# Linear attention and two feed-forwards: halves by batch, y written to the input tile by 32-column matmuls

## The chip, the cores and the metric

One core of a Trainium2 chip. The metric is the device time of one launch in microseconds (us), as the median of several runs; below one per cent, two such medians of this kernel can hardly be told apart.

## The reference, cut to what matters

```python
for t in range(S):                                   # S = 768, 4 batches, 8 heads, 48 channels
    state = alpha[:, :, t, :, None] * state + np.einsum('bhd,bhe->bhde', k[:, :, t], v[:, :, t])
    y[:, :, t] = np.einsum('bhd,bhde->bhe', q[:, :, t], state)
...
h = x @ w_in                                         # x: y as 3072 tokens x 384; w_in 384 x 2048, float64
g = (a[0] + a[1]*h + a[2]*h*h + a[3]*h**3) / (1.0 + np.abs(b[0])*np.abs(h) + np.abs(b[1])*h*h + 1e-6)
x = g @ w_out                                        # 2048 x 384
...
h = x @ w_in2                                        # 384 x 1024, then softmax times h, a norm, and @ w_out2
```

## The kernel before, in words

The sequence is cut into 6 chunks of 128 steps. Attention works on a chunk in two halves, `i = 2c + g`: in half `g` stand four of the eight heads, of all four batches. For a half, `a_dve` (halves 2 to 11; `a_turn` for halves 0 and 1) makes q and k scaled by the running product of alpha, on VectorE (DVE), and sends them through DRAM (`qk_d`, `kb_d`) to `qks` and `kns`. Then `a_pe` runs on TensorE (PE), head pair by head pair (`p` = 0, 1): scores `sc` (L396), copied and masked to `A` (L403, L404); y from the state matrix `Sbd` (L413, from chunk 1 on) and from `A` and v (L421, heads at output columns 0 and 64); at the end of the half the state update `u` (L446). A matmul of float32 is two instructions in the trace, so 4 matmuls of L413 are 8 there.

y lies head by head in PSUM, with 48 rows of every 64 in use. The feed-forward wants the 384 features in order on partitions, as three tiles `xt` of 128. So L427 and L428 copy y to `xp` as a high and a low part, and DMAs put its rows where they belong: in chunk 0 directly into `xt` (`x_put`, L533), later into a DRAM array `y_d` (L434), from which `x_load` (L540) fills `xt` when the chunk's feed-forward begins. `xt` has one buffer.

The first feed-forward runs in steps `u`, 16 a chunk, 96 in all: `m_up` does 9 matmuls of 512 columns (L555) to `hp`, then a rational function on ACT, DVE and POOL, and `m_down` 9 matmuls (L601) four steps later. Its weights come as float64 and are converted on DVE, three instructions a tile (L491, L494, L495), for the first 16 steps; the tiles `st` and `lent` hold what is loaded. The second feed-forward (L677, L741) begins in the last chunk.

Half `i` = 2c+2 and 2c+3 of attention runs between the steps of chunk c, so halves 4 to 11 run in chunks 1 to 4. The order of instructions on each engine is fixed when the program is built, by a scheduler that simulates it; each engine then works through its list in order. All DMAs are issued by one queue, SP's, in order too: one that waits holds up those behind it.

Of the kernel before, what the change touches and what calls it, by code (L numbers as in the profile page):

```python
# [30 lines left out]
def kernel(  # L31
# [41 lines left out]
    GQ = 0  # L73
# [34 lines left out]
    def consts():  # L108
        """|b1| h^2 + |b0| |h| + QC and |a3| h^2 + s a2 h + s a1 (s the sign of a3) as (root x + beta)^2 + rest."""
# [29 lines left out]
    def network(fast):  # L139
        # ------------------------------------------------------------ attention  # L140
# [6 lines left out]
        if fast:  # L147
# [19 lines left out]
            S_c = ap_.tile([128, 2, B * 2, D], F32, name="S_c")  # L167
            Sbd = ap_.tile([128, 2, B * 2, 128], F32, name="Sbd")

        def clear():  # L170
            nc.gpsimd.memset(d1, 0.0)
            nc.gpsimd.memset(_view(d1[:], 0, [[PER, NB6 + 1]]), 1.0)
            nc.gpsimd.memset(d2, 0.0)
            nc.vector.memset(alT[:, NB6 * PER:], 0.0)
            nc.vector.memset(_view(alT[:], 0, [[PER, NB6 + 1]]), 0.0)
# [45 lines left out]
        def watch(i, ra):  # L221
            jk = ap_.tile([128, 16 * D], BF16, name="jk", tag="R")
# [11 lines left out]
        def a_load(i):  # L234
            c, g = divmod(i, 2)
            if i == 1:
                own = {
                    n: borrow(3, 2048 + 1024 * x, [16 * D + 16]) for x, n in enumerate(("ra", "rk", "rq"))
                }
            for src, nm in ((alpha, "ra"), (k, "rk"), (q, "rq")):  # L240
                t = own[nm] if i == 1 else ap_.tile([128, 16 * D + 16], F32, name=nm, tag=nm)
                if i < NPE:
                    nc.gpsimd.memset(t[:, 16 * D:], 1.0)
                for b in range(B):
                    nc.sync.dma_start(  # L245
                        out=t[32 * b:32 * b + 32, :16 * D].rearrange("p (h x) -> p h x", h=4),
                        in_=src[b, 4 * g:4 * g + 4, CH * c:CH * c + CH, :].rearrange("h (j r) d -> j h (r d)", r=4),
                    )
                raws[i, nm] = t
                yield  # L250

        def a_move(i):
            c, g = divmod(i, 2)
# [22 lines left out]
        def a_dve(i):  # L276
            ra = raws.pop((i, "ra"))
            watch(i, ra)
            transpose_in(ra, alT[:], 1, 3 * PER, PER)
            yield  # L280
# [13 lines left out]
            nc.vector.tensor_tensor(qv[1], qv[1], _view(R[:], 0, [[3 * PER, 2], [PER, 3], [1, CH]]), ALU.mult)  # L294
            yield
            kb = ap_.tile([128, 4, 192], F32, name="kb", tag="R")
            for p in range(2):
                nc.vector.transpose(
                    out=_view(kb[:], 96 * p, [[32, 3], [192, 4], [1, 32]]),
# [4 lines left out]
                out=kb_d[:].rearrange("b (j r) x -> (b j) (r x)", r=4), in_=kb[:].rearrange("p r x -> p (r x)")  # L304
# [9 lines left out]
        vns = {}  # L314

        def v_load(i):
            c, g = divmod(i, 2)
            vn = vns[i] = (
                borrow(2, 1024, [B * 192 + 16]) if i == 1
                else ap_.tile([128, B * 192 + 16], F32, name="vn", tag="vn", bufs=1)  # L320
            )
            nc.gpsimd.memset(vn[:, B * 192:], 0.0)
            for b in range(B):
                nc.sync.dma_start(
                    out=vn[:, 192 * b:192 * b + 192].rearrange("p (h d) -> p h d", h=4),
                    in_=v[b, 4 * g:4 * g + 4, CH * c:CH * c + CH, :].rearrange("h t d -> t h d"),
                )

        def a_turn(i):
# [15 lines left out]
            for p in range(2):  # L345
                al = turn(ra, p)
                P = ap_.tile([128, B, CH], F32, name="Pp", tag="P")
                R = ap_.tile([128, B, CH], F32, name="Rp", tag="R")
# [38 lines left out]
        def a_pe(i):  # L387
            c, g = divmod(i, 2)
            vt = vns.pop(i)
            hf = half(i)  # L390
            for p in range(2):
                at = []
                sc = [ps_ap.tile([128, B, CH], F32, name="sc", tag="at") for j in range(2)]
                for b in range(B):
                    for j in range(2):
                        nc.tensor.matmul(  # L396
                            sc[j][:, b, :],
                            lhsT=hf.k[p][64 * j:64 * j + D, b, :], rhs=hf.q[p][64 * j:64 * j + D, b, :],
                            start=True, stop=True,
                        )  # L400
                for j in range(2):
                    t = ap_.tile([128, B, CH], F32, name="A", tag=f"A{j}")
# [5 lines left out]
                    at.append(t)  # L408
                yield
                y = ps_ap.tile([128, B, CH], F32, name="y", tag="at")  # L410
                if c:
                    for b in range(B):
                        nc.tensor.matmul(  # L413
                            y[:, b, :], lhsT=Sbd[:, g, 2 * b + p, :], rhs=hf.q[p][:, b, :],
                            start=(b == 0), stop=False, skip_group_check=True,
                        )
                M = D if c else 64
                for b in range(B):
                    for j in range(2):
                        o = 192 * b + 96 * p + 48 * j  # L420
                        nc.tensor.matmul(  # L421
                            y[64 * j:64 * j + M, b, :], lhsT=vt[:, o:o + M], rhs=at[j][:, b, :],
                            start=(c == 0 and b == 0), stop=(b == B - 1), skip_group_check=True,
                        )
                xp = ap_.tile([128, 2, NTOK], F32R, name="xp", tag="xp")
                yf = y[:].rearrange("p b t -> p (b t)")
                nc.scalar.activation(xp[:, 0, :], yf, AF.Copy)  # L427
                marks[i, p] = nc.vector.tensor_tensor(xp[:, 1, :], yf, xp[:, 0, :].bitcast(F32), ALU.subtract)  # L428
                for j in range(2):
                    r0 = 192 * g + 96 * p + 48 * j  # L430
                    if c == 0:
                        x_put(xp, j, r0)
                        continue
                    nc.sync.dma_start(  # L434
                        out=y_d[c][r0:r0 + D, :],
                        in_=xp[64 * j:64 * j + D].rearrange("p a t -> p (a t)").bitcast(F32),
                    )
                yield
# [3 lines left out]
            for b in range(B):  # L442
                for p in range(2):
                    for j in range(2):
                        o = 192 * b + 96 * p + 48 * j
                        nc.tensor.matmul(  # L446
                            u[64 * j:64 * j + 64, 2 * b + p, :], lhsT=hf.kn[:, o:o + 64], rhs=vt[:, o:o + D],
                            start=True, stop=True, skip_group_check=True,
                        )
            if c < NCH - 1:  # L450
                Ab = hf.ends
                Sg = S_c[:, g].rearrange("p (b w) e -> p b w e", b=B)
                if c:
                    nc.vector.tensor_tensor(S_c[:, g], S_c[:, g], u, ALU.add)
                    nc.gpsimd.tensor_tensor(Sg, Sg, Ab, ALU.mult)
                else:
# [567 lines left out]
```

## Time and profile before

| what | value |
|---|---|
| runs shown | 832.57, 827.46, 832.26 us; median 832.26 |
| profiled execution, first to last instruction | 830.2 us |
| PE busy | 775.5 us (93%) |
| DVE, ACT, POOL busy | 77%, 68%, 43% |
| DMA | 118.95 MB, 52% of 16 engines' span |
| mean granted PE clock | 0.952 |

The profiled execution is 2.1 us shorter than the median of the runs. Busy time of PE is a modelled figure: matmuls overlap, and the start of the next one tells more than the length of one.

### The profile page before, as it was taken

How to read it: one execution, taken by the hardware profiler on the slowest of the kernel's cores; microseconds unless marked ns; L12 is line 12 of the kernel's file. 1: busy time of each engine (PE TensorE's matmuls, PEld its weight loads, DVE VectorE, ACT ScalarE, POOL GpSimd, SP SyncE). 2: the span in 40 equal slices, each digit the busy share in tenths (PEclk: the TensorE clock that was granted, in tenths of full speed). 3: DMA queues.
4: the chain of work that ended last, by engine and by line, in shares of the span. 5: the costliest groups of instructions: out<-in, count | busy, mean ns of one | idle time of the engine just before them, and what ended most of it. 6: DMA issues, size and time to landing. Idle time of an engine off the chain costs nothing.

```text
span 830.2 us, 12585 instructions
## 1 busy us (share of the span) xinstructions
PE 775.5 (93%) x4274; PEld 640.3 (77%) x4274; DVE 635.5 (77%) x1088; ACT 564.4 (68%) x1005; POOL 357.6 (43%) x298
## 2 busy tenths in 40 slices
PE   5884989799999999989999999999999999999986
PEld 4763867577777777777777878888888989999986
DVE  6897989989597978868797966466886799776730
ACT  2334767578778787859869787798886555455541
POOL 3245767766554354433444433242224515343331
PEclk9876879899999999989999999999999999999998
DMA  7889573573848494655648160650012643632552
GB/s 170 222 202 231 169 193 103 162 212 101 223 155 202 159 246 129 201 142 175 173 119 257 54 158 20 250 210 16 1 39 78 150 98 89 151 88 70 129 123 61
DMA packets 92201, 118.95 MB, mean 143 GB/s; under 512 B 34400, under 2 KB 63072, under 8 KB 92128
## 3 DMA queue, kind: packets, MB, share of 16 engines
q1 hardware_dynamic: 92128, 118.07, 51.9%
q8 instruction: 35, 0.57, 0.3%
q14 instruction: 38, 0.31, 0.1%
HBM read 68.46 MB, written 35.42 MB: 125 GB/s over the span
## 4 chain that ended last, share of the span: by engine, by line
PE 57%; DVE 16%; DMA 12%; SPq 6%; issue 4%; ACT 3%; POOL 2%; ACTq 0%; DVEq 0%; POOLq 0%
PE x2p L601 16%; PE hp L555 16%; PE h L677 8%; PE op L741 7%; DMA qks<-qk_d 4%; PE sc L396 4%; PE y L421 2%; DMA xt<-xp 2%; SPq L245 1%; PE y L413 1%; SPq L727 1%; DVE ft L494 1%; DMA st<-in_moe_w_out_dram 1%; DVE room L717 1%; ACT jk L702 1%
## 5 line engine op out<-in xcount | busy, mean ns | idle before, releaser
L555 PE MATMUL hp<-xt,g 128*128 128x512 f32 x720 | 194.3, 416 | 17.8 <-DMA xt<-xp 12.8
L589 POOL TENSOR_TENSOR gl<-p,gh 128x512 fp32r<-128x512 f32 x96 | 131.3, 1369 | 182.0 <-ACT gh L588 121.5
L601 PE MATMUL x2p<-gh,g 128*128 128x512 f32 x576 | 198.1, 403 | 0.0
L555 PEld LDWEIGHTS hp<-xt,g 128*128 128x128 f32 x720 | 141.2, 200 | 52.9 <-issue 9.2
L601 PEld LDWEIGHTS x2p<-gh,g 128*128 128x128 f32 x576 | 108.1, 190 | 26.7 <-issue 2.5
L601 PE MATMUL x2p<-gl,g 128*128 128x512 f32 x288 | 114.7, 398 | 0.0
L741 PE MATMUL op<-w2oh,room 128*128 128x384 f32 x384 | 102.9, 342 | 2.9 <-ACT room L732 2.2
L733 POOL TENSOR_TENSOR room<-room,room 128x1024 fp32r<-128x1024 f32 x22 | 53.7, 2441 | 102.2 <-ACT room L732 98.7
L584 DVE SCALAR_TENSOR_TENSOR w<-w,co,hp 128x512 f32<-128x512 f32 x84 | 61.9, 738 | 46.6 <-ACT hp L583 46.6
L677 PE MATMUL h<-w2ih,x 128*128 128x512 f32 x288 | 90.2, 392 | 0.0
L560 ACT ACTIVATE ah<-hp 128x512 f32<-128x512 f32 x96 | 56.9, 593 | 46.7 <-PE hp L555 45.5
L563 ACT ACTIVATE w<-ah,co 128x512 f32<-128x512 f32 x96 | 78.1, 813 | 4.4 <-DVE p L579 2.6
L581 DVE SCALAR_TENSOR_TENSOR p<-p,co,hp 128x512 f32<-128x512 f32 x84 | 61.7, 735 | 24.1 <-ACT p L562 23.9
L562 ACT ACTIVATE p<-hp,co 128x512 f32<-128x512 f32 x96 | 74.3, 774 | 1.3 <-POOL gl L589 1.3
L741 PEld LDWEIGHTS op<-w2oh,room 128*128 128x128 f32 x384 | 71.1, 191 | 4.4 <-ACT room L732 2.6
L588 ACT ACTIVATE gh<-p 128x512 fp32r<-128x512 f32 x96 | 60.1, 627 | 13.3 <-PE x2p L601 8.8
L396 PEld LDWEIGHTS sc<-qks 48*128 48x128 f32 x352 | 45.3, 205 | 30.7 <-issue 22.4
L396 PE MATMUL sc<-qks 48*128 48x128 f32 x352 | 56.1, 309 | 12.1 <-DMA qks<-qk_d 11.9
L741 PE MATMUL op<-w2ol,room 128*128 128x384 f32 x192 | 65.6, 341 | 0.0
L601 PEld LDWEIGHTS x2p<-gl,g 128*128 128x128 f32 x288 | 54.5, 189 | 12.5 <-issue 1.1
L586 DVE SCALAR_TENSOR_TENSOR p<-p,co,hp 128x512 f32<-128x512 f32 x84 | 62.0, 738 | 1.3
L677 PEld LDWEIGHTS h<-w2ih,x 128*128 128x128 f32 x288 | 53.9, 188 | 10.7
(173 smaller groups left out, 1423.6 us busy)
## 6 DMA issues: line engine op xcount, KB each, us to landing
room<-room SPq DMA_DIRECT2D x96, 128.0 KB
qk_d<-qk SPq DMA_DIRECT2D x10, 771.0 KB
st<-in_moe_w_in_dram SPq DMA_DIRECT2D x15, 512.0 KB
st<-in_moe_w_out_dram SPq DMA_DIRECT2D x20, 384.0 KB
y_d<-xp SPq DMA_DIRECT2D x40, 192.0 KB
xt<-y_d SPq DMA_DIRECT2D x12, 512.0 KB
qks<-qk_d SPq DMA_DIRECT2D x20, 257.0 KB
x_d<-x2e SPq DMA_DIRECT2D x18, 256.0 KB
```

The lines of the kernel that those rows point to most:

```text
L396: nc.tensor.matmul(sc[j][:, b, :], lhsT=hf.k[p][64 * j:64 * j + D, b, :], rhs=hf.q[p][64 * j:64 * j + D, b, :], start=True, stop=True,)
L555: nc.tensor.matmul(hp, lhsT=w[:, kt, 128 * o:128 * o + 128], rhs=xts[c, kt][:, xx, :], start=(kt == 0 and w is hi and xx == 0), stop=(kt = ...
L562: nc.scalar.activation(p, hp, AF.Square, bias=co[:, 7:8], scale=co[:, 5:6])
L563: nc.scalar.activation(w, ah, AF.Square, bias=co[:, 6:7], scale=co[:, 4:5])
L581: nc.vector.scalar_tensor_tensor(p, p, a1, hp, ALU.add, ALU.mult)
L584: nc.vector.scalar_tensor_tensor(w, w, rest, hp, ALU.add, ALU.mult)
L586: fin[u] = nc.vector.scalar_tensor_tensor(p, p, a0, hp, ALU.add, ALU.mult)
L588: nc.scalar.activation(gh, p, AF.Copy)
L589: nc.gpsimd.tensor_tensor(gl, p, gh[:].bitcast(F32), ALU.subtract)
L601: nc.tensor.matmul(x2ps[c][d], lhsT=w[:, o, 128 * d:128 * d + 128], rhs=gg, start=(f == 0 and w is hi and gg is gh), stop=(f == NF1 - 1 an ...
L677: nc.tensor.matmul(hp[:, 512 * n:512 * n + 512], lhsT=x2s[c][kt][:, x, CH * b:CH * b + CH], rhs=w2[w][:, kt, 512 * n:512 * n + 512], start ...
L741: nc.tensor.matmul(op, lhsT=x[:, 128 * f:128 * f + 128], rhs=w2[w][:, f, :], start=(f == 0 and x is hi and w == "oh"), stop=(f == NF2 - 1 ...
```

## The change

Halves are now two batches with all eight heads (`slot`), so a half yields all 384 features of 256 tokens. Scores of both head pairs come first, into four tiles `A`; then all y matmuls of the half in one block. They use 32 output columns each: a pair of heads is 96 features, three pieces of 32, and output piece `m` goes to partitions `32 (m mod 4)` of tile `m // 4`. Successive matmuls thus go to the four column groups in turn. y is then in feature order, and the copies write `xt` directly, which holds all three tiles and has two buffers. `xp`, `x_put`, `y_d` in the fast path and `x_load` go. v gets 64 columns a head with zeros behind the 48. The state lives in the diagonal blocks of `Sbd` (`S_c` goes, and the two ACT copies of L459), so the DVE and POOL updates are done in two pieces of 48 partitions. To make room, `R` and `kb` lie in `alT`, `rq` shares a tile with `ra` and is loaded after `ra` was transposed, and `jk` shares the tile of `qk`.

```diff
+        def slot(i, x):
+            c, bp = divmod(i, 2)
+            return c, 2 * bp + x // 2, 4 * (x % 2)
...
         def a_dve(i):
             ra = raws.pop((i, "ra"))
+            nc.vector.memset(_view(alT[:], PER, [[PER, NB6], [1, 2]]), 0.0)
             watch(i, ra)
             transpose_in(ra, alT[:], 1, 3 * PER, PER)
+            _run(a_load(i, ("rq",)))
...
-            R = ap_.tile([128, NB6 * PER], F32, name="R", tag="R")
-            nc.vector.tensor_tensor_scan(R[:, ::-1], alT[:, 2:][:, ::-1], d2[:, ::-1], 0.0, ALU.mult, ALU.add)
+            R = alT[:, 2:]
+            nc.vector.tensor_tensor_scan(R[:, ::-1], R[:, ::-1], d2[:, ::-1], 0.0, ALU.mult, ALU.add)
...
+            y2 = [ps_ap.tile([128, n, 2 * CH], F32, name="y", tag="at") for n in (2, 1)]
+            begun = set()
+            def put(m, x, w, r, last):
+                kt, quad = divmod(m, 4)
+                first = (kt // 2, quad) not in begun
+                begun.add((kt // 2, quad))
+                nc.tensor.matmul(
+                    y2[kt // 2][32 * quad:32 * quad + 32, kt % 2, CH * x:CH * x + CH], lhsT=w, rhs=r,
+                    start=first, stop=last, skip_group_check=True,
+                )
+            pairs = range(H // 2)
+            for x in range(2):
                 if c:
+                    for hp in pairs:
+                        g, p = divmod(hp, 2)
+                        for z in range(3):
+                            put(
+                                3 * hp + z, x, Sbd[:, bp, 2 * (2 * x + g) + p, 32 * z:32 * z + 32],
+                                hf.q[p][:, 2 * x + g, :], False,
+                            )
+                for part in ((0, 1, 3), (2,)):
+                    for hp in pairs:
+                        g, p = divmod(hp, 2)
+                        for z in part:
+                            o = 512 * x + 128 * hp + (0, 32, 48, 80)[z]
+                            put(
+                                3 * hp + (0, 1, 1, 2)[z], x, vt[:, o:o + 32], A[p, z // 2][:, 2 * x + g, :], z != 1
+                            )
+            xt = x_tile(c)
+            for z, n in enumerate((2, 1)):
+                hi, lo = (xt[:, 2 * z:2 * z + n, w, 256 * bp:256 * bp + 256] for w in range(2))
+                nc.scalar.activation(hi, y2[z], AF.Copy)
+                marks[i, z] = nc.vector.tensor_tensor(lo, y2[z], hi.bitcast(F32), ALU.subtract)
...
+                xts[c] = moe_pool.tile([128, KT, 2, NTOK], F32R, name="xt", tag="xt", bufs=2)
...
-                if f == 0 and c:
+                if f == 0 and c and not fast:
                     x_load(c)
```

The order on PE, at the end of half 3's y in chunk 0. Before: y of the second head pair, cut in two, and the state update `u` around its second part.

```order
L555 MATMUL hp<-xt,g_738 128x512 x9
L413 MATMUL y<-qks,Sbd 128x128 x4
L421 MATMUL y<-A,vn 48x128
L601 MATMUL x2p_1083<-gl,g_612 128x512
L601 MATMUL x2p_1083<-gh,g_612 128x512
L601 MATMUL x2p_1081<-gh,g_738 128x512
L601 MATMUL x2p_1081<-gl,g_738 128x512
L446 MATMUL u<-vn,kns 64x48 x11
L421 MATMUL y<-A,vn 48x128 x7
L446 MATMUL u<-vn,kns 64x48 x5
L601 MATMUL x2p_1081<-gh,g_738 128x512
```

The same half's y now:

```order
L604 MATMUL x2p_1113<-gh,g_619 128x512
L422 MATMUL y<-qks,Sbd 32x128 x12
L422 MATMUL y<-A,vns 32x128 x16
L422 MATMUL y<-qks,Sbd 32x128 x12
L422 MATMUL y<-A,vns 32x128 x16
L558 MATMUL hp<-xt,g_735 128x512 x9
```

All 56 y matmuls of the half stand together, where before each head pair had its own stretch, cut once or twice. Over halves 4 to 11 the attention matmuls stood in 75 separate blocks between feed-forward matmuls, and now in 57.

The order on SP's queue during chunk 0, while half 1 is finished and half 2 made. Before (`lent` and `st` are the landing tiles of the float64 weights):

```order
L488 DMA st<-in_moe_w_out_dram 128x384
L533 DMA xt<-xp 48x1024
L533 DMA xt<-xp 16x1024
L533 DMA xt<-xp 32x1024
L303 DMA kb_d<-kb 128x768
L245 DMA rq<-in_q_dram 32x4x192 x2
L258 DMA kns<-kb_d 128x4x192
L245 DMA rq<-in_q_dram 32x4x192
L488 DMA lent_176<-in_moe_w_in_dram 128x512
L311 DMA qk_d<-qk 128x3x514
L488 DMA st<-in_moe_w_out_dram 128x384
L533 DMA xt<-xp 48x1024 x2
```

And now:

```order
L501 DMA st<-in_moe_w_out_dram 128x384
L251 DMA rk<-in_k_dram 32x4x192
L310 DMA kb_d<-alT 128x768
L501 DMA lent_173<-in_moe_w_in_dram 128x512
L251 DMA ra<-in_alpha_dram 32x4x192
L263 DMA kns<-kb_d 128x4x192
L501 DMA st<-in_moe_w_out_dram 128x384
L251 DMA ra<-in_alpha_dram 32x4x192 x3
L318 DMA qk_d<-qk 128x3x514
L501 DMA lent_173<-in_moe_w_out_dram 128x384
L501 DMA st<-in_moe_w_in_dram 128x512
```

The `xt<-xp` rows, and what they waited for, are gone; the weight loads stand in their place.

And on DVE, between half 2 and half 3 of the new order (`alT` is now also `kb`, the source of the DMA `kb_d<-alT`):

```order
L305 STREAM_TRANSPOSE alT<-qk 128x3x4x32 x2
L276 STREAM_TRANSPOSE qk<-rq 128x4x32 x2
L508 SCALAR_TENSOR_TENSOR ft<-lent_173,ft 128x512
L507 SCALAR_TENSOR_TENSOR ft<-st,ft 128x512
L271 STREAM_TRANSPOSE qk<-rq 128x2x4x32
L508 SCALAR_TENSOR_TENSOR ft<-st,ft 128x512
L283 MEMSET alT 128x6x2
L504 TENSOR_SCALAR ft<-lent_173 128x512
```

The memset of `alT` opens half 3, and it waits until the DMA has read half 2's `kb` from there; before, `alT` and `kb` were two tiles.

## Rows read from the trace of the kernel before

**Rows 1.** The page: busy time of each engine.

```profile
PE 775.5 (93%) x4274; PEld 640.3 (77%) x4274; DVE 635.5 (77%) x1088; ACT 564.4 (68%) x1005; POOL 357.6 (43%) x298
```

**Rows 2.** Busy time of each engine by stretch: length, engines (instructions), granted PE clock, DMA share, GB/s.

```profile
40.00:60.00 20.00, 14.49 (x76) 11.43 (x77) 19.22 (x34) 7.27 (x16) 9.49 (x8) 0.67 0.88 201
60.00:80.00 20.00, 10.26 (x64) 7.95 (x63) 14.68 (x25) 10.41 (x20) 8.80 (x6) 0.67 1.00 236
...
200.00:544.00 344.00, 338.61 (x1944) 267.46 (x1943) 270.02 (x424) 277.33 (x479) 145.00 (x129) 0.99 0.59 170
12.00:200.00 188.00, 154.42 (x955) 124.01 (x952) 168.69 (x288) 113.00 (x211) 107.87 (x92) 0.83 0.68 177
```

**Rows 3.** The chain that ended last, 36 to 80 us: start, length, what.

```profile
36.75 0.66 DVE xp L428
...
37.44 6.29 DMA xt<-xp
...
61.87 0.68 DVE xp L428
...
63.54 8.28 DMA xt<-xp
...
71.88 7.04 DMA lent<-in_moe_w_out_dram
```

**Rows 4.** Waits of PE, then of DVE, 12 to 200 us: total, times, longest.

```profile
PE hp L555 <- DMA xt<-xp: 12.8, 2, 7.6
...
DVE ft L491 <- DMA lent<-in_moe_w_out_dram: 3.4, 1, 3.4
...
DVE ft L491 <- DMA st<-in_moe_w_out_dram: 1.7, 2, 1.0
DVE ft L491 <- DMA lent<-in_moe_w_in_dram: 1.7, 1, 1.7
```

**Rows 5.** PE in order of time: one head pair's y, and a lone y matmul.

```profile
323.52 0.39 PE L601 MATMUL x2p<-gh,g 128*128 128x512 f32 x1
323.75 1.05 PE L413 MATMUL y<-qks,Sbd 128*128 128x128 f32 x8
324.73 1.08 PE L421 MATMUL y<-A,vn 128*48 128x128 f32 x16
325.74 0.50 PE L601 MATMUL x2p<-gl,g 128*128 128x512 f32 x1
326.08 0.63 PE L601 MATMUL x2p<-gh,g 128*128 128x512 f32 x2
...
201.84 0.42 PE L421 MATMUL y<-A,vn 128*48 128x128 f32 x2
202.19 0.50 PE L601 MATMUL x2p<-gl,g 128*128 128x512 f32 x1
```

**Rows 6.** PE in order of time: the state update, 64 columns by 48.

```profile
344.97 1.02 PE L446 MATMUL u<-vn,kns 128*64 128x48 f32 x26
345.91 0.50 PE L601 MATMUL x2p<-gh,g 128*128 128x512 f32 x1
```

**Rows 7.** Groups by line and shape: busy, mean ns of one.

```profile
L428 DVE TENSOR_TENSOR xp<-y,xp 128x512 fp32r<-128x512 f32 x24 | 16.4, 682 | 4.1 <-ACT xp L427 4.0
...
L454 DVE TENSOR_TENSOR S_c<-S_c,u 128x384 f32<-128x384 f32 x8 | 4.4, 547 | 3.4 <-PE u L446 3.4
```

**Rows 8.** DMA issues between 20 and 80 us: KB each, and the moved total.

```profile
DMA packets 13659, 13.21 MB, mean 220 GB/s; under 512 B 6229, under 2 KB 10869, under 8 KB 13654
...
xt<-xp SPq DMA_DIRECT2D x6, 192.0 KB
...
xt<-xp SPq DMA_DIRECT2D x2, 128.0 KB
...
xt<-xp SPq DMA_DIRECT2D x2, 64.0 KB
```

**Rows 9.** SP's queue in order of time: half 2's kb written, then read back.

```profile
55.87 0.53 SPq L303 DMA_DIRECT2D kb_d<-kb  x1
...
59.69 0.39 SPq L258 DMA_DIRECT2D kns<-kb_d  x1
```

More of the change, by code (lines that the diff above doesn't have):

```diff
@@ L72 @@
     NA = 5
-    GQ = 0
     PRE = (1, 1, 0, 0)
@@ L173, in clear @@
             nc.gpsimd.memset(d2, 0.0)
-            nc.vector.memset(alT[:, NB6 * PER:], 0.0)
-            nc.vector.memset(_view(alT[:], 0, [[PER, NB6 + 1]]), 0.0)
+            nc.vector.memset(alT[:, 0:1], 0.0)
         lent = {}
@@ L232, in watch_end, with a_load @@
             )
[L234 to L241, printed above, removed]
+        def slot(i, x):
+            c, bp = divmod(i, 2)
+            return c, 2 * bp + x // 2, 4 * (x % 2)
+        def a_load(i, names=("ra", "rk", "rq")):
+            for x, (src, nm) in enumerate(((alpha, "ra"), (k, "rk"), (q, "rq"))):
+                if nm not in names:
+                    continue
+                if i == 1:
+                    t = borrow(3, 2048 + 1024 * x, [16 * D + 16])
+                elif i == 0 and nm == "rq":
+                    t = borrow(3, 5120, [16 * D + 16])
+                else:
+                    t = ap_.tile([128, 16 * D + 16], F32, name=nm, tag="rk" if nm == "rk" else "ra")
                 if i < NPE:
                     nc.gpsimd.memset(t[:, 16 * D:], 1.0)
-                for b in range(B):
+                for y in range(B):
+                    c, b, h = slot(i, y)
                     nc.sync.dma_start(
-                        out=t[32 * b:32 * b + 32, :16 * D].rearrange("p (h x) -> p h x", h=4),
-                        in_=src[b, 4 * g:4 * g + 4, CH * c:CH * c + CH, :].rearrange("h (j r) d -> j h (r d)", r=4),
+                        out=t[32 * y:32 * y + 32, :16 * D].rearrange("p (h x) -> p h x", h=4),
+                        in_=src[b, h:h + 4, CH * c:CH * c + CH, :].rearrange("h (j r) d -> j h (r d)", r=4),
                     )
@@ L303, in a_dve @@
             nc.sync.dma_start(
-                out=kb_d[:].rearrange("b (j r) x -> (b j) (r x)", r=4), in_=kb[:].rearrange("p r x -> p (r x)")
+                out=kb_d[:].rearrange("b (j r) x -> (b j) (r x)", r=4), in_=R[:, :768]
             )
@@ L313, in a_dve @@
             yield
-        vns = {}
+        vts = {}
         def v_load(i):
[L317 to L323, printed above, removed]
+            vn = vts[i] = borrow(2, 1024, [B * 256]) if i == 1 else vns
+            if i < NPE:
+                nc.vector.memset(_view(vn[:], D, [[64, 4 * B], [1, 16]]), 0.0)
+            for x in range(2):
+                c, b, h = slot(i, 2 * x)
                 nc.sync.dma_start(
-                    out=vn[:, 192 * b:192 * b + 192].rearrange("p (h d) -> p h d", h=4),
-                    in_=v[b, 4 * g:4 * g + 4, CH * c:CH * c + CH, :].rearrange("h t d -> t h d"),
+                    out=vn[:, 512 * x:512 * x + 512].rearrange("p (h d) -> p h d", h=H)[:, :, :D],
+                    in_=v[b, :, CH * c:CH * c + CH, :].rearrange("h t d -> t h d"),
                 )
@@ L425, in a_pe @@
[L425 to L437, printed above, removed]
@@ new lines, in a_pe @@
+            pairs = range(H // 2)
+            for x in range(2):
+                if c:
+                    for hp in pairs:
[13 more added lines that the diff above has]
+                            )
@@ L654, in open2 @@
             pool = ph2["pool"].__enter__()
-            ph2["x"] = [pool.tile([128, 2, NTOK], F32R, name=f"x5{kt}", tag=f"x5{kt}") for kt in range(KT)]
             for nm, dims in (("i", [128, KT, DF2]), ("o", [128, NF2, DM])):
@@ L811, in half_steps @@
             gp = a_pe(i)
-            gd = chain(a_prep(i + 1), a_load(i + 2) if i + 2 < NH and i + 1 >= NPE else iter(())) if i + 1 < NH else iter(())
+            gd = chain(a_prep(i + 1), a_load(i + 2, ("ra", "rk")) if i + 2 < NH and i + 1 >= NPE else iter(())) if i + 1 < NH else iter(())
             while True:
```

115 lines of the change are left out of this document (42 added, 73 removed).

## The prediction

> **What bounds the kernel now.** I read the page first, then the table by stretch, then the chain and the waits of the opening, and last the order of time on PE. The page says PE is busy 93% of the span, DVE 77% [rows 1]. That is a mean over two regimes, and the table by stretch parts them [rows 2]. From 200 to 544 us, where attention halves 4 to 11 run beside the feed-forward, PE is busy 338.6 of 344 us at a clock of 0.99, with DVE at 78%: there PE is the bound, and what the change takes from PE comes off the end. From 12 to 200 us PE is busy 154 of 188 us at a clock of 0.83, and DVE 168.7: there DVE, which converts the weights, is the bound, and PE waits now and then. At 60 to 80 us even DVE falls to 14.7 of 20 us while the DMA engines are at 1.00: that is the one stretch in which transfers set the pace.
>
> The chain shows what happens there [rows 3]. The second piece of y is ready at 36.75 + 0.66 us, but reaches `xt` only 6.3 us later; the last piece of half 1 is ready at 62.55 (61.87 + 0.68), and its DMA takes 8.28 us more, in a queue full of weights, before the third tile of `xt` is there. The weights behind it, issued at 71.88, take 7.04 us to land. PE stood still 12.8 us for these two DMAs, and DVE 6.8 us (3.4 + 1.7 + 1.7) for weights [rows 4].
>
> **The steady part: PE.** Before, a half from chunk 1 on has two stretches like the one at 323.75 us [rows 5]. L413 holds PE from 323.75 to 324.73, 0.98 us; L421 from there to 325.74, 1.01 us; and the first 512-column matmul behind it holds PE 0.34 us (325.74 to 326.08), where the one at 323.52 held it 0.23, so 0.11 more. Sum 2.10 us, twice a half: 4.2 us.
>
> The eight instructions of L413 took 0.98 us, 0.12 us each. The sixteen of L421 took 1.01 us in all: its two heads, at output columns 0 and 64, ran side by side, and a pair costs what one instruction of the full array costs. Take the last instruction's 0.28 us tail away ((1.08 - 0.28) / 7), and a pair comes every 0.11 us. The change has 24 matmuls from the state and 32 from `A` a half, 56 matmuls or 112 instructions, against 24 matmuls or 48 instructions before. They go round four column groups. If four run side by side as two do now, that is 28 groups at 0.11 us: 3.1 us. To this come the way into and out of the block: the lone y matmul at 201.84 held PE 0.35 us for one pair worth 0.11, so 0.24, and 0.11 on the matmul behind it. 3.1 + 0.35 = 3.4 us, against 4.2: **0.8 us less a half**, 6.4 us over the 8 halves.
>
> No row shows four groups at once, so this needs bounds. From above: the state update, whose instructions are small as well, issues 26 in 0.94 us, 36 ns each [rows 6]. At that rate the block takes 112 x 0.036 + 0.35 = 4.4 us, 0.2 us more than before. Farther up, if only two ran together, 56 x 0.11 + 0.35 = 6.5 us, 2.3 us more. From below nothing goes under the 3.1 us of four side by side, since each group still streams 128 columns. I take four side by side, because L421 is the nearest row: same moving operand, same length, column groups of one array. The state update's rate may be its own weight loads.
>
> The second term on PE is the way in and out of blocks. Over halves 4 to 11 the order has 75 attention blocks before and 57 after. I have counted two of them a half before and one after in the y terms, 16 and 8; of the others, 59 become 49. Ten fewer at about 0.3 us (0.35 by the lone matmul, a little less where score matmuls stand there): **3.0 us less**; between 0 and 6, as a block may cost nothing where PE waits anyway or up to twice that in front of 9 matmuls. The scores and the state update keep their matmuls.
>
> **The opening: DMA and DVE.** The ten puts into `xt` move 6 x 192 + 2 x 128 + 2 x 64 KB, 1.54 MB, of 13.21 MB at 220 GB/s [rows 8]: 7.0 us of the queue. Without them the weights come sooner, and DVE's 6.8 us of waiting for weights can go. The first complete `hp` is also some 8 us earlier, but DVE was busy 33.9 of 40 us there, so an earlier `hp` only helps where DVE had nothing else: PE's 12.8 us are not the gain. DVE's new work takes some back. A state update on DVE, 0.55 us, becomes two [rows 7]; the instructions have the same number of elements a partition, so I give each the full 0.55. The low parts of y cost 0.68 us per 512 columns, and a half has 768 instead of 1024, so 0.34 less. The memset of 12 elements is about 0.1. Net +0.3 us a half, for the halves 0 to 5 that run in a DVE-bound stretch about 2 us. The memset also waits for the `kb_d` DMA, with weight conversions queued behind it on DVE; that DMA was issued at 55.87 and read back from 59.69 on, 3.8 us [rows 9], and five DVE instructions of some 0.6 us stand between: 1 us, once, for half 3. All in all 6.8 - 2 - 1: **4 us less**; bounds 3 us more (no wait goes, the work stays) and 12.8 us less (all that PE waited).
>
> **What costs nothing.** From 200 us on the same +0.3 us a half on DVE lies in 22% of idle time, ACT is relieved by two copies and a quarter of the y copies, and POOL, with two small multiplies where one was, is busy 145 of 344 us. If DVE's cover were gone it would be 2.4 us over 8 halves. The `y_d` traffic disappears, and with it SP's waits for `xp`; nothing on PE waited for it after 200 us, as the feed-forward of a chunk could always be filled with the matmuls of the one before. The later load of `rq` is a new wait for SP: it waits for the transposes of `ra` and for the ACT pass over it, with the next `rk` and weight loads behind it. In the opening some ten DVE instructions stand between those transposes and the first use of `rq`, and in the steady part a half lasts 43 us (344 / 8), so I cost it at zero.
>
> **Sum.** 830.2 - 6.4 - 3.0 - 4 = 816.8 us for a profiled execution, and with the 2.1 us by which the median lies above it, **819 us**. Its own range is 810 to 826: the blocks give 3 us either way, the opening some 5.
>
> **The rivals.** *The opening pays in full* (chance 0.12). PE's two waits are on the chain [rows 3], and if DVE catches up in the time in which the DMA engines are now freer, all 12.8 us go: 832.3 - 9.4 - 12.8 = 810 us. Against it stands DVE at 90% over the whole opening [rows 2].
>
> *Nothing much* (0.20). The transfers were hidden behind DVE, so the opening gives 0, and the small instructions issue at the state update's 36 ns, so y costs 0.2 us more a half, 1.6 us; the fewer blocks give 3.0 back: 831 us. For it: DVE's share, and that row. The Trainium skill says something of the kind: in "TensorE: Matmul & The Clock Gate", Part 3, three column tiles side by side reached 2.38 times the speed of one and not three. By that the 3.1 us would be 3.9, y would cost what it did, and an otherwise unchanged sum would be near 825 us. The pair in the trace shows no such loss, 0.11 us a pair against 0.12 for one instruction of the full array; no row here shows more than two tiles.
>
> *The 32-column matmuls don't run four at a time* (0.13), the way to slower. One mechanism, on PE, in all halves: with two at a time a half costs 2.3 us more, 18.4 over eight; less 3.0 for blocks and 4 for the opening that is 11 us more, 844 us. It decides from 0.17 us a group of four on (8 x (28 x 0.17 + 0.35 - 4.2) is the 7 us that the other two terms give). For it: four column groups are in no row. Against it: L421, whose two groups lose nothing.
>
> **How the numbers follow.** The forecast has 0.55. One per cent is 8.3 us, about what a measurement of this kernel can tell from no change: faster means under 824, slower over 840.6. Of the forecast's 0.55, four fifths lie under 824 and the rest within 1%; of the "nothing much" 0.20 nearly all lies within; of the 0.13, some 0.11 lies over 840. Faster 0.58, same 0.30, slower 0.12. The range runs from 805, somewhat under the full opening, to 838, short of the slow case; that leaves about 0.05 below and 0.13 above.
>
> **What would show it.** In the new order of time on PE, y's 112 instructions in one stretch of about 3.4 us, starts in fours 0.11 us apart; 4.4 us would say issue rate, 6.5 two at a time. PE's wait for `xt<-xp` gone, and `hp` of step 0 complete before 65 us. DVE's waits for weight DMAs under 3 us, DMA bytes down by about 17 MB (1.5 of puts, and five chunks of 384 x 1024 x 4 bytes written to `y_d` and read again). Chunk 1's first step some 4 us earlier than before, and the steps from there on 0.15 us closer each (9.4 us over 64 steps). I would be wrong if PE shows new idle time in the opening from sc or y waiting for `qks` or `A`, or if DVE stood at the memset of `alT` for more than 3 us a half.

## The result, and the profile after

The changed kernel takes 842.34 us (median of 4; the kernel before beside it 830.26): ratio 1.014, 95% interval 1.010 to 1.018. It is slower, where 819 us was forecast. The profiled execution has a span of 840.4 us, against 830.2.

Both spans are divided where the ninth `hp` matmul of step 16 (chunk 1 begins) and of step 80 (chunk 5) starts, into the opening, chunks 1 to 4, and the rest. Before, columns as in [rows 2]:

```profile
184.90:543.80 358.90, 353.51 (x2024) 279.09 (x2023) 283.38 (x445) 290.44 (x501) 152.50 (x135) 0.99 0.57 165
543.80:830.20 286.40, 275.82 (x1324) 242.81 (x1323) 191.71 (x358) 171.76 (x314) 100.38 (x58) 0.98 0.33 88
```

After, with the opening's rows that answer to [rows 2]:

```profile
12.00:200.00 188.00, 149.55 (x1220) 118.40 (x1216) 173.40 (x302) 108.82 (x205) 110.66 (x93) 0.84 0.59 150
60.00:80.00 20.00, 13.69 (x83) 10.79 (x83) 16.95 (x31) 11.40 (x23) 7.43 (x7) 0.76 0.96 260
180.00:546.40 366.40, 350.21 (x2552) 276.00 (x2552) 289.77 (x461) 283.14 (x491) 158.80 (x137) 0.98 0.47 134
546.40:840.40 294.00, 278.39 (x1324) 243.14 (x1323) 186.67 (x358) 170.64 (x315) 99.66 (x59) 0.98 0.31 81
```

The opening is 4.9 us shorter (184.9 to 180.0), chunks 1 to 4 are 7.5 us longer, the rest 7.6. PE's idle time in chunks 1 to 4 rose from 5.4 to 16.2 us, in the rest from 10.6 to 15.6.

On PE, y itself did what was forecast. In order of time, where [rows 5] showed a head pair before, one half's y now:

```profile
290.87 0.39 PE L604 MATMUL x2p<-gh,g 128*128 128x512 f32 x1
291.19 0.87 PE L422 MATMUL y<-qks,Sbd 128*32 128x128 f32 x24
291.87 1.06 PE L422 MATMUL y<-A,vns 128*32 128x128 f32 x32
292.74 0.84 PE L422 MATMUL y<-qks,Sbd 128*32 128x128 f32 x24
293.40 1.06 PE L422 MATMUL y<-A,vns 128*32 128x128 f32 x32
294.39 1.90 PE L558 MATMUL hp<-xt,g 128*128 128x512 f32 x7
```

112 instructions in 3.20 us (291.19 to 294.39), four in 0.11 us. From the starts, the y matmuls of the eight halves in chunks 1 to 4 held PE 33.6 us before and 26.7 now. Waits of PE from 200 to 660 us, before and then after:

```profile
PE sc L396 <- DMA qks<-qk_d: 5.3, 5, 2.2
```

```profile
PE sc L401 <- DMA qks<-qk_d: 7.7, 6, 1.8
PE x2p L604 <- ACT x2e L611: 5.3, 4, 2.4
PE h L677 <- DVE sm L698: 3.3, 1, 3.3
PE hp L558 <- DVE p L589: 2.4, 3, 1.4
PE h L677 <- ACT x2e L611: 2.4, 1, 2.4
```

PE, which waited for the scores' inputs alone, now also waits for ACT and DVE in the two feed-forwards that the change didn't touch. In the opening, for [rows 4], PE's waits and DVE's, 12 to 200 us:

```profile
PE kp L373 <- DVE xt L449: 5.6, 2, 4.5
...
PE sc L401 <- DVE Sbd L472: 4.9, 2, 4.5
...
DVE ft L504 <- DMA st<-in_moe_w_in_dram: 3.0, 3, 1.7
DVE ft L504 <- DMA lent<-in_moe_w_in_dram: 2.5, 1, 2.5
DVE ft L504 <- DMA lent<-in_moe_w_out_dram: 1.9, 2, 1.6
```

The wait for `xt<-xp` is gone, DVE's for weights are not (7.4 us, before 6.8), and PE has several new ones. The two longest are shown; it also stood 3.5 us for `xt` from ACT, 2.9 for `xt` from DVE ahead of the state update, and 4.9 in y for `A` (before 1.8), which the prediction had named as a sign of being wrong.

### The profile page after: what moved, and what is told of

Its sections match the earlier page's. It is cut to its first block, busy times and chain, and to the rows that moved or that the text cites. A ratio compares the mean times of both kernels' runs of the same rounds, so it can differ in the third digit from the quotient of the medians.

```text
span 840.4 us, 13792 instructions
## 1 busy us (share of the span) xinstructions
PE 765.0 (91%) x4978; PEld 627.6 (75%) x4978; DVE 635.4 (76%) x1109; ACT 549.7 (65%) x985; POOL 361.2 (43%) x294
## 4 chain that ended last, share of the span: by engine, by line
PE 38%; DVE 28%; DMA 15%; ACT 6%; issue 6%; SPq 4%; POOL 2%; DVEq 0%; ACTq 0%; POOLq 0%
PE hp L558 10%; PE h L677 9%; PE x2p L604 9%; PE op L741 7%; DVE ft L507 3%; DVE ft L508 3%; DMA qks<-qk_d 2%; DMA qk_d<-qk 2%; DMA st<-in_moe_w_in_dram 2%; DVE ft L504 2%; DVE w L587 2%; DVE hp L588 2%; DVE p L589 2%; DMA x_d<-x2e 2%; PE sc L401 2%
## 5 line engine op out<-in xcount | busy, mean ns | idle before, releaser
L558 PE MATMUL hp<-xt,g 128*128 128x512 f32 x864 | 229.5, 410 | 13.8 <-DVE p L589 7.2
L558 PEld LDWEIGHTS hp<-xt,g 128*128 128x128 f32 x864 | 165.6, 196 | 55.4 <-DVE p L589 9.6
L592 POOL TENSOR_TENSOR gl<-p,gh 128x512 fp32r<-128x512 f32 x96 | 129.1, 1347 | 171.9 <-ACT gh L591 124.0
L677 PE MATMUL h<-w2ih,x 128*128 128x512 f32 x288 | 93.7, 405 | 7.1 <-DVE sm L698 4.6
L563 ACT ACTIVATE ah<-hp 128x512 f32<-128x512 f32 x96 | 56.5, 589 | 25.2 <-PE hp L558 24.2
L586 ACT ACTIVATE hp<-ah 128x512 f32<-128x512 f32 x84 | 50.1, 597 | 20.0 <-DVE p L584 19.0
L401 PEld LDWEIGHTS sc<-qks 48*128 48x128 f32 x352 | 38.9, 200 | 29.7 <-issue 24.3
```

Of the source, the lines that this page charges most:

```text
L558: nc.tensor.matmul(hp, lhsT=w[:, kt, 128 * o:128 * o + 128], rhs=xts[c][:, kt, xx, :], start=(kt == 0 and w is hi and xx == 0), stop=(kt = ...
L563: nc.scalar.activation(ah, hp, AF.Abs)
L592: nc.gpsimd.tensor_tensor(gl, p, gh[:].bitcast(F32), ALU.subtract)
L677: nc.tensor.matmul(hp[:, 512 * n:512 * n + 512], lhsT=x2s[c][:, kt, x, CH * b:CH * b + CH], rhs=w2[w][:, kt, 512 * n:512 * n + 512], start ...
```

## The experiments

The instruction order of each engine is laid when the kernel is built, so each edit below moves instructions elsewhere too; that is why kernels with a new order alone (another `GS`, explained under "The hold") were run. The ratios are to the kernel before, run beside each; the stretches, in us, are those of the one profiled execution. "Scan" is the mean time from the ninth `hp` matmul of a half's first step to the start of the first DVE scan of the next half's preparation, halves 4 to 10; a minus means earlier. Medians are in the text.

| kernel | ratio (95%) | opening | chunks 1-4 | rest | scan |
|---|---|---|---|---|---|
| before | 1 | 184.9 | 358.9 | 286.4 | -0.5 |
| after | 1.014 (1.010-1.018) | 180.0 | 366.4 | 294.0 | +1.1 |
| own_jk | 1.011 (1.007-1.015) | 176.1 | 362.9 | 291.4 | +2.0 |
| turn_last | 1.018 (1.011-1.025) | 181.1 | 368.2 | 293.5 | +0.7 |
| before_shared | 1.002 (0.998-1.005) | 186.0 | 353.3 | 287.4 | +1.0 |
| before_gs3 | 0.996 (0.992-0.999) | 184.8 | 356.6 | 286.0 | -6.6 |
| y_by_dram | 1.016 (1.012-1.020) | 181.8 | 367.0 | 289.2 | -1.4 |
| before_state | 1.000 (0.997-1.003) | 186.3 | 355.6 | 286.9 | -0.6 |
| before_double | 0.994 (0.991-0.997) | 179.0 | 355.2 | 288.5 | +3.0 |
| after_gs3 | 0.999 (0.996-1.002) | 179.6 | 360.4 | 288.1 | +0.1 |
| y_split | 1.001 (0.999-1.004) | 177.0 | 369.1 | 284.3 | +2.5 |
| y_split_gs3 | 0.993 (0.989-0.996) | 174.6 | 363.4 | 284.1 | -0.1 |
| spread | 1.008 (1.005-1.012) | 173.7 | 370.2 | 293.1 | +2.1 |
| before_nostate | 1.014 (1.008-1.020) | 185.2 | 368.2 | 287.7 | -1.2 |
| before_noscan | 0.996 (0.993-0.999) | 184.1 | 352.9 | 287.6 | -1.3 |
| before_nostate_gs3 | 0.995 (0.992-0.998) | 188.5 | 352.5 | 288.5 | -4.9 |
| after_noscan_gs3 | 0.994 (0.991-0.996) | 174.8 | 352.0 | 293.2 | +0.8 |
| split_gs4 | 0.980 (0.975-0.985) | 173.2 | 354.6 | 283.4 | -6.7 |
| before_gs4 | 1.003 (1.000-1.006) | 186.9 | 356.0 | 287.6 | -12.3 |
| after_gs4 | 0.987 (0.982-0.992) | 180.7 | 355.5 | 287.4 | -7.1 |

### Shared tiles, or the order

First suspicion: the scrap tile `jk` in qk's tile. ACT's wait in the new kernel, 130 to 600 us:

```profile
ACT jk L221 <- DMA qk_d<-qk: 8.5, 5, 3.5
```

**own_jk**

```
-            jk = ap_.tile([128, 16 * D], BF16, name="jk", tag="qk")
+            jk = ap_.tile([128, 16 * D], mybir.dt.float8e4, name="jk", tag="jk")
...
```

> After, with the scrap output of the alpha check in a tile of its own (one byte an element, so that it fits; the zeros that made room for it are read from d1) instead of in qk's tile. Theory S (shared tiles): ACT stood 8.5 us in 5 pieces before L221 for the DMA that empties qk, with the x2e copies queued behind it at two chunk ends; without that PE's wait of 5.3 us for x2p at chunk ends falls under 2.5 us, its wait for hp falls from 7.2 to about 4, and the time falls by 5 to 7 us to some 836. Theory O (order: the new kernel starts the next chunk without the pause that the xt load used to make, so x2p is wanted before it is emptied, whatever ACT waits for): ACT's wait at L221 goes, but x2p and hp are waited for as before, 842 within 2 us.

836.9 us: the number of theory S, not its way there; the interval overlaps that of the new kernel. The wait for qk's DMA went, but L220 (the same instruction) now waited for `ra`, and PE for `x2p` as in the new kernel:

```profile
ACT jk L220 <- DMA ra<-in_alpha_dram: 15.0, 6, 4.8
```

```profile
PE x2p L603 <- ACT x2e L610: 4.9, 4, 2.1
```

**before_shared**: the other way round, the sharing alone in the kernel before.

```
-            R = ap_.tile([128, NB6 * PER], F32, name="R", tag="R")
+            R = alT[:, 2:]
...
-            jk = ap_.tile([128, 16 * D], BF16, name="jk", tag="R")
+            jk = ap_.tile([128, 16 * D], BF16, name="jk", tag="qk")
...
-                t = own[nm] if i == 1 else ap_.tile([128, 16 * D + 16], F32, name=nm, tag=nm)
...
+                    t = ap_.tile([128, 16 * D + 16], F32, name=nm, tag="rk" if nm == "rk" else "ra")
...
```

> The kernel before, with the new kernel's sharing of tiles alone: rq in ra's tile and loaded late, R and kb in alT, the scrap output in qk's tile; y, xt, the state and the batches as before. Theory S: ACT gets the same stalls for the DMA that empties qk (8 us or more), DVE stands for alT, qks comes later, and the time rises from 830 to 835 or more. Theory O: within 2 us of 830, since the chunk ends keep their pause.

829.2 us, no difference, though ACT stood 6.7 us for the DMA that empties qk here too: theory S falls in the kernel before. With own_jk's rows, no cause was found in the sharing; in the new kernel only `jk`'s was tested.

**turn_last**

```
+                    marks["x2"] = nc.sync.dma_start(out=x2_d[c][:, d, :], in_=e)
...
+        with tc.issue_after(marks["x2"].ins):
+            n_turn(0)
```

> After, with the 16 room DMAs of the first layer-norm tile set behind the three x_d DMAs of the last chunk in SP's order (as they stood in the kernel before). Theory O: the third x2e copy at 658.5 stood for its tile behind 10.2 us of room DMAs; that wait of PE (2.4 us) and the half-clock interval behind it (about 1.7) go, 838. Rival: the room DMAs come some 4 us later and the op matmuls behind them wait as long, so nothing is won, 842 within 1.5 us; or the tail was lost in DVE's late softmax chain (3.3 us at 636), which this leaves.

844.4 us. PE's 2.4 us for `x2e` went, and PE waited for `op`'s inputs instead: the rival was right in kind, at 2 us more than it said. The tail's larger wait stayed, and a likely cause, not tested, stands in the new kernel's rows, DVE and then POOL:

```profile
626.50 0.74 DVE L712 TENSOR_TENSOR sm<-sm 128x1 f32<-128x1 f32 x1 [1.85 <-ACT sm L711]
627.28 1.22 DVE L713 SCALAR_TENSOR_TENSOR sm<-sm 128x1 f32<-128x1 f32 x1
628.54 1.21 DVE L714 SCALAR_TENSOR_TENSOR sm<-sm 128x1 f32<-128x1 f32 x1
629.79 1.74 DVE L715 TENSOR_SCALAR room<-room,sm 128x1024 f32<-128x1024 f32 x1
...
635.99 0.15 DVE L698 TENSOR_SCALAR sm<-sm 128x1 f32<-128x1 f32 x1
...
643.31 0.15 DVE L714 SCALAR_TENSOR_TENSOR sm<-sm 128x1 f32<-128x1 f32 x1
643.50 0.81 DVE L715 TENSOR_SCALAR room<-room,sm 128x1024 f32<-128x1024 f32 x1
```

```profile
625.94 1.29 POOL L644 TENSOR_TENSOR x<-x 128x512 fp32r<-128x512 f32 x1 [3.38 <-ACT x L643]
627.19 1.30 POOL L592 TENSOR_TENSOR gl<-p,gh 128x512 fp32r<-128x512 f32 x1
628.44 2.54 POOL L644 TENSOR_TENSOR x<-x 128x512 fp32r<-128x512 f32 x2
...
635.75 2.53 POOL L644 TENSOR_TENSOR x<-x 128x512 fp32r<-128x512 f32 x2 [1.17 <-ACT x L643]
```

DVE's one-element instructions with two inputs (L712 to L714), 0.15 us without company (643.31), end when POOL's do (627.24 beside 627.23, 628.50 beside 628.49), and L715 took 1.74 us for 0.81: some 3.6 us more on DVE, just ahead of the 3.3 us that PE's next `h` waited for `sm`. The one with a single input at 635.99 took its 0.15 us beside a running POOL. The four kernels with such a wait for `sm` (after, turn_last, spread, after_noscan_gs3) have a rest of 293 to 294 us, the others 283 to 291.

**before_gs3**: `GS = 2` became `GS = 3`. The expectation has it the wrong way round in words: with 3 the preparation may go one step sooner.

> The kernel before with GS = 3 for 2: the same instructions, only the next half's preparation is held back behind another step, so the whole order is laid anew. It measures what a new order alone does. Theory O: some us either way, 826 to 838. Theory S: within 2 us of 830.

825.6 us, just under both ranges: this new order is worth 0.4% in the kernel before.

### The pause at the chunk's end

**y_by_dram**

```
+            xt = ap_.tile([128, KT, 2, 256], F32R, name="xs", tag="xs") if c else x_tile(c)
...
+                nc.sync.dma_start(
...
+                    in_=xt[:, kt].bitcast(F32),
...
-                if f == 0 and c and not fast:
+                if f == 0 and c:
```

> After, with y's copies taken apart from xt again for chunks 1 to 5: they go into a staging tile, by DMA to DRAM and from there into a single xt (chunk 5's in the memory of the second feed-forward), as in the kernel before; the 32-column matmuls, the batches, the state and the shared tiles stay. Theory O (the pause at each chunk end that the xt load made kept PE far enough behind ACT and DVE): PE's waits for x2p at chunk ends (5.3 us) go, those for hp fall to 4 or less, and the time falls by 8 us or more, to 834 or under. Rival L (DVE and ACT are simply what PE waits for, now that PE has less to do): the waits stay, some at other places, and the time is 842 or, with the added transfers, some us above.

841.1 us. **before_state** (the reference) and **before_double**:

```
...
-                    nc.vector.tensor_tensor(S_c[:, g], S_c[:, g], u, ALU.add)
...
+                        nc.vector.tensor_tensor(S, S, u[rows], ALU.add)
...
```

> The kernel before with the shared tiles and with the state in its diagonal tile alone (no S_c, DVE and POOL work in two pieces of 48 rows on Sbd, no ACT copies; the identity and the zeros stand elsewhere for room). A rival T3 (two DVE pieces a half load the engine that PE waits for) expects 833 to 836; theory O nothing, 829 within 2 us. It is also the reference for the next.

```
-                moe_pool.tile([128, 2, NTOK], F32R, name="x2", tag=f"xt{kt}") for kt in range(KT)
+                moe_pool.tile([128, 2, NTOK], F32R, name="x2", tag=f"xt{kt}", bufs=2) for kt in range(KT)
```

(`xt` likewise.)

> The same as before_state, and xt doubled: the load of a chunk's xt from DRAM no longer waits for the last step of the chunk before. This is the one part of the change that takes the pause away. Theory O: it becomes slower than before_state by 5 us or more, with new waits of PE for x2p behind ACT's x2e at chunk ends. Rival L: not slower, within 2 us, or faster.

829.1 and 824.8 us. Theory O falls twice: the pause given back to the new kernel wins nothing, and the pause taken away from the kernel before loses nothing but wins 0.5% over before_state, with an opening 7.3 us shorter. Neither the state's two pieces nor the doubled `xt` costs anything.

**after_gs3**: `GS = 3`.

> After with GS = 3 for 2: the same instructions in an order laid anew, to see how far the order alone moves the new kernel. Theory O: the waits for x2p and hp stay, 838 to 846. If it falls to 830, the loss is one order's bad luck and no property of the change.

828.3 us, 14 us less with the same instructions. So the loss is in the order. In chunks 1 to 4 PE is busy for less and yet idle for longer, 23.6 us for 16.2:

```profile
179.60:540.00 360.40, 336.78 (x2551) 264.17 (x2550) 289.14 (x451) 284.07 (x490) 157.16 (x137) 1.00 0.46 134
```

### The burst of y, and the premise

**y_split**

```
+                if x == 0:
+                    yield
```

> After, with y's block of 112 instructions (3.2 us on PE without a feed-forward matmul) cut into two of 56, one a step later than the other. Theory B (burst: in these 3.2 us no new hp comes, DVE runs dry at the fifth step of a half, 0.47 busy where it was 0.70 before, and PE then stands for hp and x2p; only three hp tiles lie between them): DVE's hole in the fifth step shrinks, PE's gaps over 0.3 us beside the feed-forward in chunks 1 to 4 fall from 14.6 to under 8 us, and the time falls by 8 us or more, to 834 or under. Rival Q (the pace is DVE's queue in the first three steps, 0.93 to 0.98 busy, whatever form y has): gaps and time as in after, 842 within 3 us. Rival R (one order's luck): anything from 828 to 842, without the hole changing.

> The same with GS = 3, which lets a half's preparation on DVE go one step sooner; beside after_gs3 at 828.3. Theory B: gaps fall from 22 to under 12 us, 820 or under, and so the first that is faster than before. Rival Q: 828 within 3 us.

831.6 and 824.7 us: faster, but not for the reason given. Chunks 1 to 4 took 369.1 and 363.4 us, no less than uncut; what was won lies in the opening and the rest. Theory B falls.

**spread** (`if b != "end" and n % 2 == 0: b = next(gd, "end")`)

> After, with DVE's preparation of the next half handed out at one and two pieces a step in turn, where it was two: it takes six steps of the eight and not four. Rival Q: DVE no longer stands at 0.95 in the first three steps, PE's waits for hp get shorter, 835 or under. Theory B: y's block still starves DVE; within 3 us of 842, or slower where qks now comes late for the next half.

838.1 us, chunks 1 to 4 the longest of all; rival Q falls, and theory B's number is missed by 1 us.

**before_nostate**

```
-                if c:
+                if c < 0:
```

(with `M` and `start` as in chunk 0)

> The kernel before without y's matmuls from the state (80 matmuls; the output lacks what earlier chunks contribute): PE has 2 us less in each of 10 halves, 8 of them in chunks 1 to 4. It tests the premise of the forecast, that in the steady part what is taken from PE comes off the end. If PE is the bound there: 16 to 20 us less, 810 to 813. If ACT and DVE are right behind PE: under 8 us less, 822 or more, with PE's idle time in chunks 1 to 4 up by the rest.

842.3 us: with less for PE (the y matmuls of chunks 1 to 4 held it 21.3 us for 33.6, so 1.5 us a half and not 2), the kernel before got slower by as much as by the change. The first forecast falls; the second, 822 or more, holds but had no rise in it.

```profile
185.20:553.40 368.20, 353.44 (x1896) 270.90 (x1895) 287.02 (x446) 289.33 (x501) 150.57 (x136) 0.97 0.54 157
```

PE executes 128 instructions fewer than before in chunks 1 to 4, is busy as long as before at a granted clock of 0.97 for 0.99, and idles 14.8 us for 5.4.

### The hold

`GS` says behind which step's last DVE instruction the next half's preparation is queued on DVE: 2 steps back, 3 or 4.

**before_nostate_gs3**

> before_nostate (y's matmuls from the state left out, 2 us of PE a half) with GS = 3. Theory G: with the hold loosened the time taken from PE comes off the end at last, 812 or under, against 825.6 of before_gs3. Theory D: not faster than before_gs3, 824 to 842.

**before_noscan** and **after_noscan_gs3** (`R = alT[:, 2:]`, the scan left out):

> The kernel before without the second scan of a half's preparation (R; k is multiplied by the raw alpha instead, so the output is another): 1.77 us less on DVE in each of 10 halves, PE's work unchanged. Theory D (DVE sets the pace in chunks 1 to 4): 10 us less or more, 820 or under. Theory G (PE sets it, and the hold on the preparation spoils it): within 4 us of 830.

> after_gs3 without the same scan on DVE (here k is multiplied by the raw alpha too, so the output is another): 1.77 us less on DVE in each of 10 halves. Theory D: 10 us less or more than after_gs3, 818 or under, and more than in the kernel before, since PE has time free. Theory G: within 4 us of 828.

827.5, 826.3 and 823.7 us. Neither theory has all its numbers: the first is D's, the second G's, the third nobody's. One step of the hold took 15.7 us off chunks 1 to 4 of before_nostate (368.2 to 352.5), as G would have it; but beside before_gs3 (356.6) the work taken from PE gives only 4.1, and 14 us taken from DVE gives 6.0 (358.9 to 352.9) and 8.4 (360.4 to 352.0). Orders alone spread chunks 1 to 4 of the kernels that keep all of the kernel before's work (before, before_shared, before_state, before_double, before_gs3, before_gs4) from 353.3 to 358.9 us, so the first two gains are about as large as that spread. The rows of the last two kernels in these stretches:

```profile
188.50:541.00 352.50, 343.23 (x1860) 262.94 (x1859) 281.54 (x437) 287.75 (x497) 149.29 (x134) 0.98 0.57 165
```

```profile
174.80:526.80 352.00, 334.02 (x2549) 263.97 (x2548) 276.13 (x451) 284.56 (x492) 154.73 (x138) 1.00 0.47 139
```

PE is idle 9 and 18 us there, and ACT and DVE are some 80% busy. No kernel went under 352 us.

**split_gs4**, **before_gs4**, **after_gs4**: `GS = 4` in y_split, before and after.

> y_split with GS = 4. If the hold is what costs the new kernel its time (G), a looser one gives some us more, 820 or under, against 824.7 with GS = 3. If GS = 2 was one unlucky order, or DVE sets the pace (D), 823 to 830.

> The kernel before with GS = 4. If the looser hold helps only a kernel with less work on PE (G), the kernel before stays between 822 and 829, and split_gs4's 2% belong to the change and the hold together. If it falls to 815 or under, the hold alone gives the gain and the change is worth nothing even with the hold that suits it.

> The new kernel with GS = 4, y's block uncut. From GS = 2 to 3 it went from 842 to 828. If the hold is the whole of it, 813 to 818, beside split_gs4's 812.9, and faster than before by over 1%; if the cut of y's block matters too, as at GS = 2 and 3 (11 and 4 us), 818 to 826; if single orders decide, anything up to 835.

812.9, 830.4 and 818.5 us. The kernel before hardly cares for the hold (830, 826, 830 with 2, 3, 4); the new one does (842, 828, 818), and so it does with the cut (832, 825, 813). Chunks 1 to 4 of after_gs4 and split_gs4:

```profile
180.70:536.20 355.50, 340.04 (x2547) 268.69 (x2545) 286.60 (x451) 283.12 (x489) 159.44 (x136) 0.98 0.46 134
```

```profile
173.20:527.80 354.60, 336.22 (x2558) 263.90 (x2557) 290.29 (x460) 285.56 (x495) 159.32 (x139) 0.99 0.47 133
```

In after_gs4 the scan starts 7 us before the ninth matmul of the half's first step, with GS = 2 1 us behind it, and 11 us are gone from chunks 1 to 4. split_gs4 beats both kernels, by 2.0% (1.5 to 2.5) against before. Whether the cut of y gives something beside the hold at GS = 4 is open, as the intervals of the two kernels overlap.

Where PE's time went in chunks 1 to 4, in us: each instruction from its start to the start of the next, with PE's idle time taken out and put in a column. A few per cent of the instructions have no record, so a term is good to 1 or 2 us. The last column is the time at a granted clock of 0.50.

| kernel | y | scores | update `u` | feed-forward | idle | clock 0.50 |
|---|---|---|---|---|---|---|
| before | 33.6 | 33.6 | 9.6 | 276.7 | 5.4 | 6.8 |
| after | 26.7 | 32.1 | 8.5 | 282.9 | 16.2 | 17.1 |
| after_gs3 | 25.7 | 22.6 | 8.6 | 279.8 | 23.6 | 3.4 |
| after_gs4 | 27.1 | 23.8 | 8.5 | 280.5 | 15.5 | 13.7 |
| y_split | 28.0 | 24.2 | 9.2 | 284.1 | 23.6 | 20.5 |
| split_gs4 | 27.2 | 21.6 | 8.5 | 278.9 | 18.4 | 6.8 |
| before_nostate | 21.3 | 35.6 | 10.0 | 286.6 | 14.8 | 23.9 |
| before_nostate_gs3 | 19.8 | 32.9 | 9.5 | 281.1 | 9.3 | 13.7 |

So GS = 3 and 4 did not take the new kernel's idle time away. What fell with them is the time of the scores and the time at the lower clock. The scores are the same instructions, but eight of them can take 1.13 or 0.72 us, here in after and in after_gs3:

```profile
313.02 1.13 PE L401 MATMUL sc<-qks 48*128 48x128 f32 x8 [1.60 <-DMA qks<-qk_d]
```

```profile
312.88 0.72 PE L401 MATMUL sc<-qks 48*128 48x128 f32 x8
```

In the first they start 0.11 us apart, in the second in pairs 7 ns apart, a pair every 0.11 us. That fits the two heads of a pair in turn, where the other order has one head by itself. PE's busy time for the scores alone (PE, its weight loads, then ACT, clock, DMA share, GB/s), before, after and after_gs3:

```profile
184.90:543.80 358.90, 36.23 (x240) 28.70 (x240) 17.33 (x30) 0.99 0.57 165
```

```profile
180.00:546.40 366.40, 34.53 (x244) 26.98 (x244) 17.78 (x31) 0.98 0.47 134
```

```profile
179.60:540.00 360.40, 24.46 (x242) 18.93 (x242) 17.26 (x31) 1.00 0.46 134
```

The scores alone don't decide the time either: y_split has them at 24.2 us and took 369.1.

## Why the prediction was wrong

**The premise "there PE is the bound, and what the change takes from PE comes off the end" is the step that failed.** Its evidence was PE busy 338.6 of 344 us [rows 2]. That a stretch is full doesn't say that it gets shorter when the work does: before_nostate took more from PE than y's new form (12.3 us for 6.9 in chunks 1 to 4) and got slower. What the change takes from PE had the right size: 9.5 us (y 6.9, scores 1.5, update 1.1) where 9.4 were forecast for y and blocks. But 10.8 us came back as idle time and 6.2 in the feed-forward's own matmuls, most of that because PE was at the lower clock for 17.1 us and not 6.8; so chunks 1 to 4 became 7.5 us longer. The clock is not that of one execution alone: over all runs its mean is 0.945 in after and 0.953 in after_gs3, and 0.953 to 0.955 in the kernel before.

**What turned no gain into a loss is the order that the hold gave.** GS is the only edit between 842, 828 and 818 us, and between 832, 825 and 813 with y cut. How the order does it stays open. The scan came some 5 us early or more in five kernels, and their chunks 1 to 4 took 352 to 357 us; but before_shared, before_state, before_double, before_noscan and after_noscan_gs3 took 352 to 356 us with the scan at -1.3 to +3.0, and from after to after_gs3 it moved by 1 us only. So a late scan isn't shown to be what costs the time. From GS = 2 to 4 chunks 1 to 4 of the kernel before became 3 us shorter, those of after 11, and from 2 to 3 those of before_nostate 16. Why the two kernels with less work on PE gain more, why the waits fall on `hp` and `x2p` in the feed-forward, and what holds chunks 1 to 4 at 352 us, the runs don't settle.

**y on PE, -0.8 us a half: right.** 3.20 us for the 3.4 forecast, so 4.4 us at the state update's rate and 6.5 with two at a time are both out.

**The opening, -4: right in size (-4.9), half wrong in reason.** PE's 12.8 us for `xt<-xp` went, but DVE's waits for weights, which were to fall under 3 us, stayed at 7.4, and new waits of PE for `xt`, `Sbd` and `A` took some back. In split_gs4 the opening is 11.7 us shorter: the 12.8 us of the rival "the opening pays in full" were nearly reached there; the runs don't show why.

**"Costs nothing": right for the shared tiles, the state's two pieces (0.55 us each, 548 ns measured) and the late `rq`**, by before_shared and before_state; DMA bytes fell by 17.2 MB as forecast. Wrong for the rest of the kernel, which wasn't in the sum at all and lost 7.6 us, most of them with two waits of the new order (3.3 and 2.4 us); the wait for `sm` is absent in after_gs3 and after_gs4, where the rest took 288.1 and 287.4.

That after_gs4 stands at 818.5 us beside the forecast of 819 doesn't save the sum: chunks 1 to 4 gave it 0.5 us against before_gs4, not 9.4, the opening 6.2. Its profiled execution was the slowest of its runs, some 7 us over the median, so where the others won more can't be read.

## What to carry to other kernels

Before a full engine is called the bound, leave some of its work out and look whether the time falls; here 1.5 us a half less for PE made the kernel slower. Where the order is laid at build and holds are counted in steps, run the kernel before and the changed one at the neighbouring settings too: the same change made the time 1.4% longer at one hold and 1.4% shorter at another (818.5 beside 830.4 us with GS = 4). And take a busy stretch apart by groups, from start to start: the kernel before, 98% busy there, gave 33.6 us to scores that after_gs3 had in 22.6.

## What the runs showed of the hardware

After idle time PE worked for a while at the lower of its two clock levels, 1.2 and 2.4 GHz. The new kernel's tail, the idle stretch ahead of 636.13 us and two stretches behind it (columns as in [rows 2]):

```profile
632.80:636.10 3.30, 0.01 (x1) 0.00 (x0) 3.23 (x6) 2.59 (x5) 1.62 (x2) 1.00 0.02 7
636.90:640.30 3.40, 3.40 (x9) 2.64 (x8) 1.38 (x6) 1.65 (x4) 2.62 (x3) 0.50 0.00 0
640.40:643.80 3.40, 3.40 (x16) 2.77 (x15) 1.59 (x3) 0.37 (x1) 0.00 (x0) 1.00 0.00 0
```

Granted 0.50, PE did 9 matmuls in 3.4 us, and 16 in the next 3.4: such a wait is paid for a second time behind it, here with about 1.6 us (7 matmuls of 0.23). A shorter one in chunk 1 was followed by a fall too: PE waited 1.76 us, did the 1.95 us of work between, and then had 0.50 for 6.8 us, with 18 instructions, where the next 6.8 us had 33 (some of both are the small ones of the scores).

```profile
266.32 1.13 PE L401 MATMUL sc<-qks 48*128 48x128 f32 x8 [1.76 <-DMA qks<-qk_d]
```

```profile
268.30:275.10 6.80, 6.80 (x18) 5.36 (x18) 4.58 (x8) 2.89 (x6) 2.05 (x2) 0.50 0.01 2
275.10:281.90 6.80, 6.80 (x33) 5.12 (x32) 6.66 (x11) 5.42 (x10) 4.61 (x3) 1.00 0.44 132
```

Small matmuls on different parts of the array ran side by side: y's in fours every 0.11 us (291.19), the scores in pairs every 0.11 us (312.88), where scores of one head by themselves came singly every 0.11 us (313.02).

DVE's smallest instructions with two inputs stood until POOL's running instruction had ended (rows at 626.50); one with a single input did not (635.99). The Trainium skill's page "SBUF — State Buffer", section "SBUF: two separate sides", says that the two engines share a port pair which one of them holds for a whole instruction; for DVE it counts instructions with two inputs in SBUF among those that need the pair. The two pairs of ends above, equal within 0.01 us, agree with it, and so does the instruction at 635.99.
